# Sixteen tiles in front of a tuned spectral kernel: leftovers evicted with the pairs, seven row sums on GpSimd, a new order

## The chip, the cores and the metric

The kernel runs on one NeuronCore of a Trainium2 chip. The metric is the time of one execution on the device in microseconds (us), the median of several runs. A profiled execution is recorded beside them; the rows below are from it. The engines are TensorE (PE in the profile, its weight loads PEld), VectorE (DVE), ScalarE (ACT), GpSimd (POOL) and SyncE (SP, which here only issues DMA transfers).

## What is computed

`x` has 2048 rows (positions) of 576 columns, in fp32. Two branches read the normalised `xn`, and their sum is added to `x`:

```python
def _A_ref(x, w_r, w_i):                       # spectral filter
    X = rfft2(x, axes=(-2, -1))                # 2048 x 289 complex
    return irfft2(X * (w_r + 1j * w_i), (S, D), axes=(-2, -1))

def _B_ref(x, w_q, k1, k2, u, v):              # 32 heads, 8 x 8 experts, one expert per head
    q = einsum("nd,dhc->nhc", xf, w_q)
    s1 = einsum("nhd,ed->nhe", q[..., :dk], k1); s2 = einsum("nhd,ed->nhe", q[..., dk:], k2)
    top_e = argmax(s1) * E + argmax(s2)
    act = gelu(einsum("nd,nhkd->nhk", xf, u[top_e]))
    return einsum("nhk,nhk,nhkd->nd", g, act, v[top_e])   # g is 1

xn = _layernorm(x)
return x + _A_ref(xn, w_r, w_i) + _B_ref(xn, w_q, k1, k2, u, v)
```

## The kernel before

The two-dimensional transform is done as products. The 2048 positions are sixteen tiles of 128. For each tile `t`:

- `ln(t, n)` takes mean and variance, of some tiles on DVE (two `bn_stats` of 288 columns and a `bn_aggr`), of the tiles in `SA` on ACT (a summing pass and a squaring pass over the row), then the inverse root `r`: a square root on ACT and four small steps on DVE.
- `folds(t)` makes the difference and the sum of a row's halves (289 columns each, in `e`): the difference on GpSimd, the sum on DVE, which adds minus twice the mean. The factor `r` is multiplied into a copy of the transform matrix, `Rs` (ACT, for some tiles DVE). Columns 0 to 32, the leftovers beyond 128 pairs, are copied three times, to 99 columns (`fl`).
- `dft128(t)` multiplies: 8 products with the columns as weights give the pairs (2 x 256 columns of two PSUM banks), 4 give the leftovers (128 columns beside them, 99 partitions). In the trace a product in fp32 makes two records. Then the result is split into two fp16 parts: ACT copies it (`hi`), DVE subtracts the copy (`ab`); for the leftovers ACT copies and DVE corrects 33 partitions.

After that, `d_fwd`, `s_fwd`, `s_mul`, `s_inv`, `s_left`, `s_last` do the column transform, the step along positions, the filter and the way back for sixteen groups `g`; the transforms read the fp16 parts (`AB`, `ABL`) as weights. In the other branch `fold_part(b, s)` multiplies the keys into `w_q`, which comes from HBM in 32 pieces through five buffers; `scores`, `route`, `combine` pick the experts. `d_inv` and `fin` do the last transform and add all to `x`, which goes out from SyncE's queue.

The program first only notes the operations (`plan.add`): matmuls of one step that follow one another are one operation, everything else is one each. They are numbered as the source reaches them. `issue` then emits them in the sequence written out in `ORDER`, and `BANK` gives each PSUM tile its first bank. So `ORDER` fixes each engine's queue, and SyncE's too; an engine takes its queue strictly in that order. A GpSimd operation that reads the SBUF also waits for the DVE operation that stands last before it in `ORDER`, of those that use the port the two share (`held`, `tc.add_manual_dep`). All instructions are emitted in one line, L321, so the profile's groups are told apart by tiles: `A` is `e`, `U` is `fl`, `t` is also the scratch of the passes, `banks` all of PSUM, `c` the constants.

## Time and profile before

| | us |
|---|---|
| median of 3 runs | 206.54 (206.07 to 208.66) |
| the profiled execution | 204.99 |
| its span, first to last instruction | 203.2 |
| PE busy | 190.7 |
| DVE, ACT, POOL busy | 160.2, 124.0, 105.9 |
| granted TensorE clock, mean | 0.995 |

The span is what the engines' records cover; 1.8 us of the execution lie around it. A share of busy time is an average over stages of very different kinds, so the rows below are taken by stretch.

### The profile page before, as it was taken

To read this page: it belongs to the slowest core of one execution; us is meant where nothing else is said; L and a number is where in the kernel's file an instruction comes from. 1 tells how busy PE (TensorE), PEld (TensorE's weight loads), DVE (VectorE), ACT (ScalarE), POOL (GpSimd) and SP (SyncE) were. 2 spreads that over 40 slices of the span, in tenths; PEclk is the share of its full clock that TensorE was granted. 3 is DMA by queue.
4 is the path that set the end of the run, shared out by engine and by line. 5 is a ranking of instruction groups with operands and counts; after the bars stand their busy time and mean duration, and the time that the engine had idled before them with its cause. 6 is when DMAs were issued, how large, how long until landed. Compare 5 with 4: busy or idle time off the path is not lost.

```text
span 203.2 us, 6358 instructions
## 1 busy us (share of the span) xinstructions
PE 190.7 (94%) x2511; PEld 126.5 (62%) x2511; DVE 160.2 (79%) x383; ACT 124.0 (61%) x272; POOL 105.9 (52%) x166
## 2 busy tenths in 40 slices
PE   7877989999999999999999999999999999999990
PEld 2466777886676567754445555477444887776640
DVE  3799999855656657686989298999999989879871
ACT  3699988955646584888985851876440953333310
POOL 2563664100550063915336967752792569798841
PEclk9999999999999999999999999999999999999997
DMA  6999699999899999793566265422101000015575
GB/s 212 411 422 418 215 379 411 413 413 412 266 405 397 400 365 352 187 313 109 139 205 161 67 156 194 138 77 52 22 7 20 7 5 0 5 38 215 212 290 182
DMA packets 21156, 44.15 MB, mean 217 GB/s; under 512 B 7942, under 2 KB 10758, under 8 KB 21126
## 3 DMA queue, kind: packets, MB, share of 16 engines
q1 hardware_dynamic: 21126, 43.74, 60.5%
q8 instruction: 20, 0.33, 0.6%
q14 instruction: 10, 0.08, 0.1%
HBM read 38.30 MB, written 4.72 MB: 212 GB/s over the span
## 4 chain that ended last, share of the span: by engine, by line
PE 79%; DVE 10%; DMA 6%; issue 1%; ACT 1%; DVEq 0%; SPq 0%; ACTq 0%
PE banks L321 79%; DMA Wt<-in_W_dram 4%; DMA XN<-in_x_dram 2%; DVE st L321 2%; DVE AB L321 2%; DVE A L321 1%; DVE w L321 1%; DVE rr L321 1%; DVE t L321 1%; DVE mx L321 1%; DVE XN L321 0%; DVE Rs L321 0%; DVE mv L321 0%; DVE ABL L321 0%; ACT AB L321 0%
## 5 line engine op out<-in xcount | busy, mean ns | idle before, releaser
L321 PE MATMUL banks<-MU,xT 128*128 128x512 f16 x192 | 44.4, 379 | 0.0
L321 PEld LDWEIGHTS <-xT 128*128 128x128 f16 (+1 forms) x240 | 20.7, 99 | 27.4 <-issue 5.0
L321 PEld LDWEIGHTS <-AB 128*128 128x128 f16 x400 | 31.2, 122 | 7.4 <-issue 3.5
L321 POOL TENSOR_TENSOR U<-t,t 128x289 f32<-128x289 f32 x32 | 21.7, 703 | 22.0 <-DVE sc L321 15.7
L321 PE MATMUL banks<-c,AB 128*128 128x145 f16 (+1 forms) x384 | 32.3, 228 | 0.4 <-DVE AB L321 0.4
L321 POOL TENSOR_TENSOR t<-t,Wt 128x578 f32<-128x578 f32 x12 | 15.6, 1314 | 21.7 <-ACT t L321 16.4
L321 DVE TENSOR_TENSOR AB<-banks,AB 128x512 f16<-128x512 f32 x32 | 21.7, 681 | 5.1 <-ACT AB L321 4.7
L321 POOL TENSOR_TENSOR xT<-xf,xT 128x640 f16<-128x640 f32 x12 | 16.8, 1403 | 15.4 <-ACT xf L321 5.5
L321 POOL TENSOR_TENSOR A<-t 128x289 f32<-128x289 f32 x32 | 21.3, 699 | 2.8 <-DVE MT L321 2.5
L321 PE MATMUL banks<-Rs,A 64*128 64x128 f32 x256 | 19.1, 288 | 3.3 <-ACT Rs L321 1.4
L321 ACT ACTIVATE AB<-banks 128x512 f16<-128x512 f32 x32 | 18.9, 596 | 3.9 <-PE banks L321 3.2
L321 PEld LDWEIGHTS banks<-Rs,A 64*128 64x128 f32 x256 | 16.7, 195 | 5.8 <-ACT Rs L321 3.4
L321 PE MATMUL banks<-s,U 64*64 64x128 f32 x624 | 20.3, 272 | 0.0
L321 PEld LDWEIGHTS banks<-s,U 64*64 64x64 f32 x624 | 17.8, 133 | 2.5 <-issue 1.1
L321 PE MATMUL banks<-A,s 64*64 64x289 f32 x256 | 18.6, 408 | 0.0
L321 ACT ACTIVATE U<-banks,sc 128x290 f32<-128x290 f32 (+1 forms) x16 | 9.3, 595 | 14.3 <-PE banks L321 9.5
L321 PE MATMUL banks<-w,KP 128*32 128x288 f32 x256 | 18.0, 410 | 0.0
L321 DVE SCALAR_TENSOR_TENSOR t<-banks,wx,Wt 128x578 f32<-128x578 f32 x20 | 15.7, 813 | 2.4 <-PE banks L321 2.1
L321 PE MATMUL banks<-c,ABL 99*128 99x289 f16 (+1 forms) x64 | 15.7, 289 | 0.2 <-ACT A L321 0.2
L321 DVE SCALAR_TENSOR_TENSOR t<-banks,sc,U 128x290 f32<-128x290 f32 (+1 forms) x26 | 12.7, 532 | 3.4 <-ACT U L321 1.9
L321 ACT ACTIVATE t<-banks,wx 128x578 f32<-128x578 f32 x12 | 8.7, 743 | 10.6 <-DVE t L321 5.4
L321 ACT ACTIVATE xT<-xf,bx 128x640 f16<-128x640 f32 x16 | 13.1, 828 | 2.5 <-DMA xf<-in_xT_dram 2.3
(133 smaller groups left out, 350.5 us busy)
## 6 DMA issues: line engine op xcount, KB each, us to landing
w<-in_wq_dram SPq DMA_DIRECT2D x32, 576.0 KB
xf<-in_xT_dram SPq DMA_DIRECT2D x16, 320.0 KB
Wt<-in_W_dram SPq DMA_DIRECT2D x8, 578.0 KB
XN<-in_x_dram SPq DMA_DIRECT2D x7, 578.0 KB
out_dram<-XN SPq DMA_DIRECT2D x14, 288.0 KB
s<-in_s_dram SPq DMA_DIRECT2D x16, 192.0 KB
c<-in_c_dram SPq DMA_DIRECT2D x1, 868.5 KB
ABL<-lo SPq DMA_DIRECT2D x42, 16.5 KB
```

What stands on the lines that cost most here:

```text
L321: o.last = fn(*[x.place() if isinstance(x, _Ps) else x for x in args], **{k: x.place() if isinstance(x, _Ps) else x for k, x in kw.items()})
```

## The change

- `AB` and `ABL` become one array `ABX` of ten rows of columns: rows 0 to 3 the fp16 rests, 4 to 7 the `hi` parts, 8 and 9 the leftovers. Readers of `AB` take the other index (`1 - ha`).
- So `dft128` copies pairs and leftovers in one ACT instruction of 768 columns on all 128 partitions; the two DVE subtractions remain. A DVE fill sets the partitions 96 to 127 of the leftover columns of all eight banks to zero once, ahead of the fill of the warm-up operand; there are 14 warm-up products for 16.
- Tile 14 leaves `SA`: its statistics go from ACT to DVE.
- `GS`, empty before, holds seven tiles. For these GpSimd makes the sum of the halves, without the mean; DVE adds minus twice the mean in the 33 leftover columns alone; and in `dft128` two more products (one per half of the partitions) with minus four times the mean of each row as weights and the 64 columns of `Rs` put the mean into the pairs. `ln` makes that multiple in one more small GpSimd instruction for each of three groups.
- `ORDER` and `BANK` are written anew, 1225 operations for 1230.

These branches were in the source before and are now taken:

```python
if t in GS:                                              # folds
    G.tensor_tensor(e[:, 0], xn[:, 0:L], xn[:, L:], op=OP.add)
    V.tensor_scalar(e[:, 0, 0:33], e[:, 0, 0:33], rr[:, 2, t:t + 1], None, op0=OP.add)
...
if b == 0 and t in GS:                                   # dft128
    for h, r in enumerate(hs):
        P.matmul(p[:, h, 0:64], rr[r, 4, t:t + 1].to_broadcast([64, 128]), Rs[r, 0], start=False, stop=False,
                 tile_position=(64 * h, 0))
```

What the two orders say of some queues, decoded by numbering the operations (numbers after a name are tiles, groups or pieces):

```
ACT before  root 0 | sum 3 | square 3 | Rs 0 | root 1-3 | fl 0 | sum 7 | Rs 3 | Rs 2 | left 0 | square 7 | hi 0 | sum 5 | fl 1
            | square 5 | Rs 1 | left 3 | root 4-7 | hi 2 | sum 11 | hi 3 | Rs 4
ACT after   sum 3 | root 0 | fl 0 | square 3 | Rs 0 | root 1-3 | Rs 1 | Rs 2 | fl 1 | sum 7 | sum 5 | hi 0 | square 5 | Rs 3
            | square 7 | root 4-7 | sum 9 | hi 2 | hi 3 | Rs 4
DVE before  stats 0 | stats 2 | normalise 0 | sum 0 | stats 1 | normalise 1-3 | sums 1, 3, 2
DVE after   stats 0 | sum 0 | normalise 0, among it stats 2 | stats 1 | normalise 1-3, among it 33 columns of 3 and 2 | sum 1
PE before   tiles 0, 3, 2, 1, 4, 6, 5 | fold products x3 | tile 7 | x2 | tiles 9, 10, 8 | x3 | tiles 11, 13, 12, 14, 15
PE after    tiles 0, 1, 2, 3 | fold products x2 | tiles 4, 6, 7 | x2 | tile 5 | x1 | tiles 8, 9 | x3 | tiles 10 to 15
DVE before, at the end of the way back   si 12 | wt 7 | si 13 | rt | cb | rt | si 15 | rt | si 14 | two leftovers
DVE after                                si 12 | wt 7 | si 13 | cb | rt | si 15 | si 14 | rt | two leftovers
last additions before   tile 14 second half | tile 15 second half | tile 15 first half
last additions after    tile 15 second half | tile 15 first half | tile 14 second half
```

In DVE's new queue the statistics of tile 14 stand ahead of the subtraction of tile 5. The diff, without the tables of `ORDER` and `BANK` (the lines above tell of them) and the like edits of the readers:

```diff
-    AB = K([128, 2, 4, S], F16, "AB")
-    ABL = K([128, 2, S], F16, "ABL")
+
+    ABX = K([128, 10, S], F16, "AB")
+    AB = ABX[:, 0:8].rearrange("p (q c) s -> p q c s", q=2)
+    ABL = ABX[:, 8:10]
     U = K([128, 2316], F32, "U")
     slots["y"], slots["es"] = ([U[:, 579 * i:579 * i + 578] for i in range(4)], [U[:, 580 * i:580 * i + 580] for i in range(2)])
     turn["y"] = turn["es"] = 0
...
     ABt = AB.rearrange("p q c (n t) -> p q c n t", t=16)
     ABLt = ABL.rearrange("p b (n t) -> p b n t", t=16)
     ABi = AB.rearrange("p q c (a e g m) -> p q (c a) g e m", a=2, g=16, e=2)
-    wu = AB[:, 0, 0, 0:512]
+    wu = AB[:, 1, 0, 0:512]
     V.memset(wu, 1.0)
+
+    V.memset(banks.rearrange("p (k c) -> p k c", c=512)[96:128, :, 256:384], 0.0)
     pw_ = PS("m", (128, 512))
-    for k in range(16):
+    for k in range(14):
         P.matmul(pw_, wu[:, 0:128], wu, start=True, stop=True)
 
     MU = K([128, 2, 4, 512], F16, "MU")
...
             v = v.unsqueeze(2).to_broadcast([128, k, 2])
         V.tensor_scalar(dst.bitcast(I32), v, 0.5, float(0x1FBD1DF5 + (e << 23)), op0=OP.mult, op1=OP.add)
 
-    SA = (3, 5, 7, 9, 11, 13, 14, 15)
+    SA = (3, 5, 7, 9, 11, 13, 15)
     rr = K([128, 5, 16], F32, "rr")
     mv = K([128, 16, 2], F32, "mv")
     eps = K([128, 1], F32, "eps")
...
 
     FF = {}
     FG, RV = range(2, 16), (5, 7, 9, 11, 13, 14, 15)
-    GS = ()
+    GS = (2, 3, 4, 5, 6, 8, 10)
 
     @staged
     def folds(t):
...
             for h, r in enumerate(hs):
                 P.matmul(p[:99, h, 256 + 64 * b:320 + 64 * b], fl[r, b], Rs[r, 0], start=True,
                          stop=True, tile_position=(64 * h, 0))
-        m = p[:, :, 0:256].rearrange("p h (n r) -> p n h r", r=2)
-        l = p[:, :, 256:384].rearrange("p h (n r) -> p n h r", r=2)
-        hi, ab = (AB[:, q].rearrange("p c (h n) -> p (c h) n", n=64)[:, :, 4 * t:4 * t + 4].rearrange("p n (h r) -> p n h r", r=2)
-                  for q in range(2))
+        m = p[:, :, 0:384].rearrange("p h (n r) -> p n h r", r=2)
+        lo, hi, fl = (ABX[:, k:l].rearrange("p c (h n) -> p (c h) n", n=64)[:, :, 4 * t:4 * t + 4].rearrange("p n (h r) -> p n h r", r=2)
+                      for k, l in ((0, 4), (4, 10), (8, 10)))
         A.activation(hi, m, AF.Copy)
-        V.tensor_tensor(ab, m, hi, op=OP.subtract)
-        lo = ABL.rearrange("p b (h n) -> p (b h) n", n=64)[:, :, 4 * t:4 * t + 4].rearrange("p n (h r) -> p n h r", r=2)
-        A.activation(lo[:99], l[:99], AF.Copy)
-        V.tensor_tensor(lo[:33], l[:33], lo[:33], op=OP.subtract)
+        V.tensor_tensor(lo, m[:, 0:128], hi[:, 0:128], op=OP.subtract)
+        V.tensor_tensor(fl[:33], m[:33, 128:192], fl[:33], op=OP.subtract)
 
 
     uv = K([128, 4], F32, "uv")
...
-                    P.matmul(p[:, b, cs], ABg[:, ha, 2 * b + c, place[g], :], dc[:, b, hb, cs], start=False,
+                    P.matmul(p[:, b, cs], ABg[:, 1 - ha, 2 * b + c, place[g], :], dc[:, b, hb, cs], start=False,
...
-        hi, ab = (ABi[:, q, :, g] for q in range(2))
+        ab, hi = (ABi[:, q, :, g] for q in range(2))
```

## Rows read from the trace of the kernel before

**Rows 1.** Part 1 of the page: busy us, share of the span, instructions.

```profile
PE 190.7 (94%) x2511; PEld 126.5 (62%) x2511; DVE 160.2 (79%) x383; ACT 124.0 (61%) x272; POOL 105.9 (52%) x166
```

**Rows 2.** Busy time by stretch: length, each engine, granted clock, DMA share, GB/s.

```profile
0.00:7.84 7.84, 6.08 (x16) 2.11 (x17) 3.85 (x14) 3.83 (x8) 2.69 (x9) 1.00 0.79 281
7.84:17.48 9.64, 6.24 (x96) 5.61 (x96) 8.84 (x30) 8.16 (x24) 5.52 (x18) 1.00 1.03 420
17.48:26.64 9.16, 8.58 (x137) 6.70 (x137) 8.71 (x26) 9.13 (x26) 5.75 (x13) 1.00 0.83 305
26.64:61.20 34.56, 34.53 (x563) 27.15 (x563) 24.15 (x68) 23.32 (x56) 11.01 (x24) 1.00 0.99 384
61.20:73.40 12.20, 11.55 (x196) 7.57 (x192) 8.35 (x21) 8.39 (x18) 0.74 (x1) 1.00 1.03 403
73.40:157.20 83.80, 83.74 (x922) 47.74 (x922) 69.92 (x156) 54.12 (x103) 48.85 (x54) 1.00 0.49 144
157.20:163.40 6.20, 5.75 (x167) 4.87 (x166) 6.17 (x12) 5.28 (x16) 3.51 (x7) 1.00 0.05 8
197.40:203.20 5.80, 0.24 (x2) 0.00 (x0) 1.37 (x3) 0.40 (x1) 0.80 (x1) 0.81 0.53 194
```

**Rows 3.** The same view inside 20 to 25 us.

```profile
20.00:22.50 2.50, 2.47 (x46) 2.06 (x46) 2.50 (x8) 2.50 (x7) 2.33 (x7) 1.00 0.75 307
22.50:25.00 2.50, 2.50 (x48) 1.75 (x40) 2.39 (x9) 2.47 (x9) 1.04 (x2) 1.00 0.60 125
```

**Rows 4.** Groups of instructions by form: busy us, mean ns | idle before, releasers.

```profile
L321 ACT ACTIVATE AB<-banks 128x512 f16<-128x512 f32 x32 | 18.9, 596 | 3.9 <-PE banks L321 3.2 <-DVE ABL L321 0.3
...
L321 ACT ACTIVATE ABL<-banks 99x256 f16<-99x256 f32 x18 | 6.5, 381 | 0.7 <-PE banks L321 0.6
...
L321 POOL TENSOR_TENSOR A<-XN 128x289 f32<-128x289 f32 x16 | 11.2, 708 | 4.8 <-DMA XN<-in_x_dram 4.1 <-DVE A L321 0.4
...
L321 DVE SCALAR_TENSOR_TENSOR A<-XN,rr 128x289 f32<-128x289 f32 x16 | 8.1, 530 | 0.3 <-POOL rr L321 0.2
...
L321 PE MATMUL banks<-Rs,U 64*99 64x64 f32 x128 | 7.8, 243 | 1.0 <-POOL U L321 0.6 <-ACT U L321 0.4
...
L321 DVE BATCH_NORM_STATS2 st<-XN 128x6 f32<-128x288 f32 x16 | 6.6, 446 | 3.0 <-DMA XN<-in_x_dram 3.0
...
L321 ACT ACTIVATE t<-XN,rr 128x576 bf16<-128x576 f32 x8 | 6.2, 778 | 0.1
...
L321 ACT ACTIVATE t<-XN 128x576 bf16<-128x576 f32 x8 | 5.5, 688 | 0.4 <-DMA XN<-in_x_dram 0.4
...
L321 DVE TENSOR_SCALAR Rs<-c,rr 128x128 f32<-128x128 f32 x7 | 2.5, 352 | 0.0
...
L321 DVE MEMSET AB<- 128x512 f16 x1 | 0.5, 485 | 0.1
```

**Rows 5.** Timeline of the first tiles, ACT and PE: start, length, instruction, [idle before].

```profile
4.77 0.30 ACT L321 ACTIVATE rr<-mv,eps 128x1 f32<-128x1 f32 x1 [2.55 <-DVE mv L321]
...
5.46 0.68 ACT L321 ACTIVATE t<-XN 128x576 bf16<-128x576 f32 x1 [0.39 <-DMA XN<-in_x_dram]
...
7.84 1.22 PE L321 MATMUL banks<-Rs,A 64*128 64x128 f32 x16 [0.28 <-DVE A L321]
...
17.48 1.22 PE L321 MATMUL banks<-Rs,A 64*128 64x128 f32 x16 [1.43 <-ACT Rs L321]
...
21.85 1.66 PE L321 MATMUL banks<-w,KP 128*32 128x288 f32 x24
```

**Rows 6.** Timeline of PE, two groups of 32 spectral products.

```profile
67.55 2.89 PE L321 MATMUL banks<-A,s 64*64 64x289 f32 x32
...
140.04 2.13 PE L321 MATMUL banks<-A,s 64*64 64x289 f32 x32
```

**Rows 7.** Timeline of PE at the first inverse column product.

```profile
163.36 0.88 PE L321 MATMUL banks<-c,AB 128*128 128x145 f16 x10 [0.45 <-DVE AB L321]
```

**Rows 8.** Timeline of DVE, the last additions.

```profile
197.43 1.37 DVE L321 SCALAR_TENSOR_TENSOR XN<-banks,sc,XN 128x289 f32<-128x289 f32 x3 [0.68 <-PE banks L321]
```

More of the change, by code (lines that the diff above doesn't have):

```diff
@@ L956, in d_inv @@
                 for n, (ha, hb) in enumerate(((0, 0), (0, 1), (1, 0))):
-                    P.matmul(p[:, b, cs], ABt[:, ha, 2 * c + b, :, t], ic[:, b, hb, cs], start=(c == n == 0), stop=False)
+                    P.matmul(p[:, b, cs], ABt[:, 1 - ha, 2 * c + b, :, t], ic[:, b, hb, cs], start=(c == n == 0), stop=False)
         plan.cut()
```

127 rows, old and new, of tables (BANK, ORDER) are left out of this document.

## The prediction, made before the changed kernel was run

> **What bounds the kernel now.** I read first the busy times, then the busy time by stretch, then the chain of waits and the stretches in which TensorE (PE) stood still. PE is busy for 94% of the span [rows 1]. Cut where its work changes kind, the stretches show where the other 6% lies [rows 2]: before the first product of a tile at 7.84 us it runs only its 16 warm-up products; from 7.84 to 17.48 it stands for 3.40 us, to 26.64 for 0.58, to 61.2 for 0.03; 0.65 in 61.2 to 73.4, 0.45 in 157.2 to 163.4, and 5.56 at the end. So after 7.84 us there are 5.1 us in all to be won inside the kernel, and the sixteen tiles (normalise, fold, transform) hold 4.0 of them. In that stage PE waits for VectorE (DVE) and ScalarE (ACT), which feed it: DVE is busy 8.84 of 9.64 us and then 8.71 of 9.16, ACT 8.16 and 9.13, GpSimd (POOL) only 5.52 and 5.75 [rows 2]. From 17.48 on all three are near their limit, so one relieved by a little does not free the others. The DMA is full (shares above 1) up to 73 us except for a hole at 20 to 25 us, where 307 and 125 GB/s stand against 420 [rows 2, 3]: SyncE waits there for a buffer of the fold products.
>
> **Leftovers evicted with the pairs.** Removed are sixteen ACT copies of 99x256 at 0.381 us; the pair copies grow from 512 to 768 columns. From 0.381 at 256 and 0.596 at 512 columns [rows 4] the line leads to 0.81, so a tile saves 0.596 + 0.381 - 0.81 = 0.17 us, 2.7 us in all. That is the upper end: where ACT's instructions follow one another closely their ends overlap, and only the columns count; the lower end is nothing. It lies on ACT, in a stage where DVE is as full. Against it the pair copy now waits for the four leftover products of its tile (0.49 us, [rows 4]: 7.8 us for sixteen tiles) where it waited for the other eight alone. DVE's two subtractions stay as they are.
>
> **One zeroing of PSUM, two warm-ups fewer.** DVE fills 1024 columns of 32 partitions before the warm-up operand. By the 0.485 us of a 512-column fill [rows 4] that is 1.0 us, twice that at worst. DVE has nothing to do before 3.7 us, so it costs nothing there; the warm-ups start 1.0 us later, and 14 instead of 16 (6.08 us together, [rows 2]) end near 7.8. The first tile's product, below, comes later than that. Without this cover it would cost the 0.2 us by which they end later.
>
> **Statistics of tile 14 from ACT to DVE.** ACT loses 0.688 + 0.778 = 1.5 us, DVE gains two statistics of 0.446 and a small closing one, 1.1 us [rows 4].
>
> **Seven row sums on GpSimd.** DVE drops seven adds of 0.530 us for seven additions over 33 columns; those cost between nothing and the 0.352 of a 128-column one [rows 4], I take 0.25, near the latter's fixed part: 7 x 0.28 = 2.0 us saved, 0.9 net of tile 14. POOL adds seven times 0.708 and three small ones, 5.7 us. Its 11.3 busy us of 18.8 become about 17, still less than either neighbour. The Trainium skill advises the other way: "GPSIMD Engine Reference", section 4.1, calls GpSimd about twice as slow as VectorE in a two-input elementwise operation. The rows give 0.708 against 0.530, a third more; with the factor two the POOL term would be 8 us and the queue full.
>
> PE gets two products a tile, 64 rows by 64 columns in fp32. The nearest row is the leftover product of the same width, 7.8 us for 128 records [rows 4], 61 ns each; two records a product and 28 in all make 1.7 us at most, 0 at least if the wait for an operand covers them. As the first two tiles' share falls into idle time, I take 1.3.
>
> **The new order, first tiles.** Numbering the operations shows a summing pass of tile 3 put ahead of tile 0's square root on ACT. Before, that root ran at 4.77; the pass cannot begin before its load has landed, at 5.46, and takes 0.68 [rows 5]. So the root comes at 6.2. From root to first product it was 3.07 us, of which the 0.53 of tile 0's sum is now done earlier: the first product comes near 8.75, 0.9 later. Next, what leads to tile 4's product at 17.48: between the root of tiles 1 to 3 and tile 4's scaled matrix ACT loses two leftover copies (0.76) and gains a summing pass (0.69) and three longer copies (0.6); that root itself is late by the 0.9 of tile 0, less some DVE time that the early sum frees, 0.7; so tile 4's product starts near 18.7. But two groups of fold products now stand before it in PE's queue, 0.55 us each (1.66 for three, [rows 5]). In work done PE is 0.1 us behind. From there the stage is nearly all PE's: five of the seven tiles with the new product follow, 0.9 us; of the old 0.6 us of standing I count 0.1 as recovered. The stage thus ends 0.9 us later. Its bounds: if all 4.0 us of standing went, 0.9 + 1.3 - 4.0 = 1.8 earlier; if a tile in the middle also waits for DVE to clear its bank (the order puts tile 14's statistics ahead of tile 5's subtraction, about 1 us) and nothing is recovered, 2.5 later.
>
> **The order, 61 to 73 us.** PE stands there for 0.65, and a group of 32 products that takes 2.13 elsewhere took 2.89, 0.7 more [rows 6]; the DMA is full in that stretch [rows 2], and these products and those before them read what it was still bringing. The new order frees two fold buffers earlier, which closes the hole at 20 to 25 us: (420-307)/420 x 2.5 + (420-125)/420 x 2.5 = 2.4 us of transfer time [rows 3]. With the data earlier and PE later, both waits go: -1.35. If a later buffer blocks SyncE instead, 0.
>
> **The order, from 157 us.** The subtraction for which the inverse products wait stood behind three routing steps and PE stood 0.45 for it [rows 7]; two remain ahead of it: -0.3, between 0 and the 0.45 us of the gap. In the last group of additions the one whose bank is ready first is now last, so the last three (1.37 us, [rows 8]) start when PE is fully done: +0.25, at most the length of one, 0.45. All else between is PE work in another order, 83.74 busy of 83.80 us [rows 2]: nothing to win, and nothing lost unless a bank comes free late.
>
> **Sum.** 0.9 - 1.35 - 0.3 + 0.25 = -0.5 on a profiled execution of 204.99 us: 204.5. The median of the runs is 206.54, 1.55 above that execution, so I expect 206.0 there.
>
> **Rivals.** One: ACT was the true limit of the tiles. It is the fullest engine from 17.48 to 26.64 (9.13 of 9.16), and it is relieved by up to 4.2 us. Then the standing time goes and the sum is -1.8 - 1.35 - 0.3 = -3.45: 203.1. Against it speaks that DVE is as full and is relieved by only 0.9.
>
> Two, slower: GpSimd becomes the limit. Each tile's fold copy now waits for a GpSimd difference, a GpSimd sum, and a DVE step between, and a GpSimd operation that uses the common port is held in the code until the DVE operation before it in the order is done. It decides as soon as a sum ends after PE has reached that tile: each such tile then costs 0.7 us. With five tiles (4, 5, 6, 8, 10) that is 3.5 us, and the DMA waits come back only in part: +3.5 - 0.5 = 209.5. For it: 17 of 18.8 us is full for a queue that already stood waiting for DVE. Against it: the tile order puts sums two tiles ahead of their use. The Trainium skill, "SBUF — State Buffer", section "Who interferes with whom", says that a VectorE instruction with two SBUF inputs and a GpSimd one that reads SBUF block each other for a whole instruction. Here GpSimd's adds of the tiles last 0.708 on average [rows 4] beside a DVE that is busy nine tenths of the time, which leaves no room for frequent blocking of that kind.
>
> Three: one array now holds pairs and leftovers, and if the waits went by array instead of by region, inverse and forward products would wait for transfers of leftovers that they don't read. Seven such steps, each priced like the one gap of that kind, 0.45 [rows 7], give +3.2 - 0.5: 209.2. The old array already mixed regions that different steps write, without such waits, so this is unlikely.
>
> **How the numbers follow.** The forecast (about 0.5 faster, within 1.5 us) has 0.68, the first rival 0.16, the second 0.13, the third 0.03. The range takes in the first rival and nearly reaches the second: 203.0 to 209.0. A change of 2% is 4.1 us, about what a measurement can tell here. Faster by more needs the first rival and luck beside it: 0.04; slower by more (210.7) needs two of the slower ones together, or more tiles than five: 0.07; within: 0.89.
>
> **What would show it.** In the changed trace: the first tile product near 8.7 and tile 4's near 18.7; the last tile done near 40.5; ACT copies of 768 columns near 0.81 us; GpSimd adds still near 0.70; no hole in the DMA at 20 to 25 us; the group of 32 products before 70 us at 2.13; the gap at 163 gone. I am wrong if PE stands on GpSimd in the tiles, or if PE is never idle from 10 us on.

## The result, and the profile after

The changed kernel takes 207.75 us in the median of 22 runs (206.1 to 210.84), the kernel before 206.5 us beside it (22 runs, 204.79 to 209.29). The ratio is 1.0049 with a 95% interval of 1.0026 to 1.0071: about 1.0 us slower, where 0.5 us faster was forecast. It is less than the 1.25 us between the medians because the slow runs of both kernels are left out of it. The time lies inside the predicted range and inside 2%, but on the other side of no change. The profiled execution spans 204.6 us, against 203.2.

Part 1 of the page of the changed kernel answers to [rows 1]:

```profile
PE 190.7 (93%) x2537; PEld 127.3 (62%) x2537; DVE 162.7 (79%) x387; ACT 119.9 (59%) x252; POOL 112.7 (55%) x175
```

The work moved as intended: ACT has 4.1 us less, GpSimd 6.8 more. PE is as busy as before: the new products (0.17 us a tile in its timeline) are about made up for by the two warm-ups that are gone (5.12 us for 6.08). DVE has 2.5 us more, where the prediction's terms (2.0 less for the sums, 1.1 more for tile 14, 1.0 for the fill) leave it about even; the section on the middle comes back to it. What was lost is standing time of PE. The same stretches as in [rows 2]:

```profile
7.84:17.48 9.64, 7.15 (x116) 6.55 (x120) 7.50 (x28) 7.19 (x20) 6.62 (x18) 1.00 1.02 420
17.48:26.64 9.16, 7.67 (x126) 6.30 (x118) 9.02 (x29) 7.31 (x18) 6.73 (x16) 1.00 0.86 322
...
61.20:73.40 12.20, 12.20 (x224) 9.02 (x222) 7.43 (x18) 10.31 (x22) 1.55 (x3) 1.00 0.99 361
73.40:157.20 83.80, 82.11 (x912) 45.62 (x910) 70.61 (x148) 53.83 (x104) 49.79 (x53) 1.00 0.50 152
157.20:163.40 6.20, 6.13 (x157) 4.67 (x159) 6.10 (x16) 3.57 (x11) 2.38 (x4) 1.00 0.05 8
```

From 61.2 to 73.4 us PE doesn't stand at all now (0.65 before), and that part came as predicted. From 73.4 to 157.2 it stands for 1.69 us, where it had stood for 0.06. PE's timeline of the changed kernel names the places:

```profile
9.06 1.22 PE L320 MATMUL banks<-Rs,A 64*128 64x128 f32 x16 [1.38 <-ACT Rs L320]
...
19.15 0.51 PE L320 MATMUL banks<-Rs,A 64*128 64x128 f32 x4 [1.20 <-DVE AB L320]
...
68.75 2.61 PE L320 MATMUL banks<-A,s 64*64 64x289 f32 x32
...
80.50 0.69 PE L320 MATMUL banks<-w,KP 128*32 128x288 f32 x8 [1.01 <-DMA w<-in_wq_dram]
...
126.80 1.98 PE L320 MATMUL banks<-s,U 64*64 64x128 f32 x64 [0.48 <-DVE t L320]
...
136.27 0.38 PE L320 MATMUL banks<-wm,on 128*128 128x2 f32 x2 [0.20 <-ACT t L320]
...
164.25 0.27 PE L320 MATMUL banks<-id,MT 128*128 128x128 f16 x2 [0.19 <-DVE AB L320]
164.85 2.38 PE L320 MATMUL banks<-c,AB 128*128 128x145 f16 x28 [0.33 <-DVE AB L320]
```

The first and second rows answer to [rows 5] (first tile 7.84, tile 4 17.48), the third to [rows 6], the last to [rows 7]. To say where the difference of 1.4 us between the spans arises, the starts of the same work in both timelines are compared:

| stretch | before | after | change |
|---|---|---|---|
| last tile product ends at | 39.64 | 40.75 | +1.1 |
| first product of the scores starts at | 87.69 | 88.79 | +1.1 (nothing more) |
| from there to the third transpose of the combines | 69.37 | 70.15 | +0.78 |
| third to eighth transpose | 37.56 | 38.00 | +0.44 |
| PE's end to the end of the span | 5.56 | 4.64 | -0.92 |

From the eighth transpose to PE's end both take 3.02 us. The sum is 1.1 + 0.78 + 0.44 - 0.92 = 1.4. This is one profile of each kernel; what further profiles of the same orders make of it is told with the experiments.

The groups of instructions by form (busy us, mean ns) answer to [rows 4]:

```profile
L320 ACT ACTIVATE AB<-banks 128x768 f16<-128x768 f32 x16 | 12.5, 804 | 1.7 <-PE banks L320 1.6
...
L320 POOL TENSOR_TENSOR A<-XN 128x289 f32<-128x289 f32 x23 | 15.8, 698 | 9.3 <-DVE A L320 3.2 <-DMA XN<-in_x_dram 2.8 <-PE banks L320 1.5
...
L320 DVE TENSOR_SCALAR A<-A,rr 128x33 f32<-128x33 f32 x7 | 1.9, 279 | 0.0
```

The 768-column copy takes 0.804 us (0.81 estimated), a GpSimd addition 0.698 (0.70), the 33-column addition 0.279 (0.25). The prices of the operations were right. What failed lies between them.

### The profile page after: what moved, and what is told of

It reads as the page before. It is cut to its first block, busy times and chain, and to the rows that moved or that the text cites. A ratio compares the mean times of both kernels' runs of the same rounds, so it can differ in the third digit from the quotient of the medians.

```text
span 204.6 us, 6425 instructions
## 1 busy us (share of the span) xinstructions
PE 190.7 (93%) x2537; PEld 127.3 (62%) x2537; DVE 162.7 (79%) x387; ACT 119.9 (59%) x252; POOL 112.7 (55%) x175
## 4 chain that ended last, share of the span: by engine, by line
PE 65%; DVE 14%; ACT 6%; DMA 5%; POOL 5%; issue 3%; POOLq 0%; SPq 0%; DVEq 0%; ACTq 0%
PE banks L320 65%; DVE w L320 6%; DMA w<-in_wq_dram 3%; ACT t L320 3%; DVE AB L320 2%; DMA XN<-in_x_dram 2%; POOL A L320 2%; DVE MT L320 1%; DVE st L320 1%; DVE mx L320 1%; POOL t L320 1%; POOL U L320 1%; DVE rr L320 1%; ACT xf L320 1%; DVE t L320 1%
## 5 line engine op out<-in xcount | busy, mean ns | idle before, releaser
L320 PEld LDWEIGHTS <-AB 128*128 128x128 f16 (+1 forms) x462 | 34.4, 123 | 8.5 <-issue 4.1
L320 PE MATMUL banks<-c,AB 128*128 128x145 f16 (+3 forms) x448 | 36.5, 236 | 0.3 <-DVE AB L320 0.3
L320 POOL TENSOR_TENSOR U<-t,t 128x289 f32<-128x289 f32 x32 | 22.6, 729 | 21.8 <-ACT A L320 14.9
L320 DVE TENSOR_TENSOR AB<-banks,AB 128x512 f16<-128x512 f32 (+1 forms) x50 | 27.8, 581 | 2.6 <-ACT AB L320 2.4
L320 ACT ACTIVATE AB<-banks 128x768 f16<-128x768 f32 (+2 forms) x34 | 22.6, 680 | 4.6 <-PE banks L320 4.5
L320 PE MATMUL banks<-Rs,A 64*128 64x128 f32 x256 | 20.7, 291 | 4.1 <-ACT Rs L320 2.6
L320 PEld LDWEIGHTS banks<-Rs,A 64*128 64x128 f32 x256 | 17.5, 194 | 6.4 <-ACT Rs L320 5.1
L320 POOL TENSOR_TENSOR A<-XN 128x289 f32<-128x289 f32 x23 | 15.8, 698 | 9.3 <-DVE A L320 3.2
L320 PE MATMUL banks<-A,s 64*64 64x289 f32 x256 | 17.7, 407 | 0.0
L320 ACT ACTIVATE A<-banks 128x578 f32<-128x578 f32 x16 | 10.4, 654 | 6.2 <-issue 4.0
```

What stands on the lines that cost most here:

```text
L320: o.last = fn(*[x.place() if isinstance(x, _Ps) else x for x in args], **{k: x.place() if isinstance(x, _Ps) else x for k, x in kw.items()})
```

## Experiments

All times are medians; each ratio is to the kernel before on the same chip, with its 95% interval. "Scores" is the start of the scores' first product. In order edits, `root(0)` and the like stand for the numbers of those operations in ORDER.

### Edits and order, taken apart

**e1**, all edits in the order of before:

```diff
  ORDER, BANK of before, and in it:
- hi(t) 512, lo(t) 256 columns        + hi(t) 768 at the later of the two places
- DVE sum(t)                          + GpSimd sum(t) behind its difference, DVE sum33(t) here
- ACT sum, square of tile 14          + DVE statistics of tile 14
```

> All four edits (wide eviction, one zeroing and 14 warm-ups, tile 14's statistics on DVE, seven sums on GpSimd with their products) in the order of before; each new instruction stands where the one that it replaces stood, a GpSimd sum right behind its tile's difference. Theory (the loss of 1.25 us is the new order's, at places that I priced at nothing): the edits cost their seven pairs of products, 1.3 us of PE, and win part of the 4.0 us of standing back: 206.0 to 207.0, no tile product waits for GpSimd, and no wait for a fold buffer of a microsecond near 80 us. Rival (the edits themselves carry the loss): 207.7 or more, with PE waiting in the tiles on GpSimd or on the wide copies.

Measured: 210.88 us, ratio 1.0203 (1.0138 to 1.0268). PE waits 1.49 us for GpSimd at 16.09, tiles end at 41.66, three waits for fold pieces make 1.76 us, the scores start at 91.92.

**e2**, the new ORDER and BANK with the operations of before:

> None of the edits, only the new order (and its banks): sums, leftover copies and tile 14's statistics stand where the new order has what replaces them. Theory: the waits that belong to the order are all there: first tile product near 9 us, 1.0 us on a transfer near 80 us, 0.5 us behind the routing steps near 127 us, and the early stores; 207.5 to 208.5, slower than before. Rival (the edits carry the loss): near 206.5, like before, since the order merely moves waits about. Second rival (the order fits only the edits): over 209, because DVE must run seven sums that the order doesn't make room for.

Measured: 210.94 us, 1.0239 (1.0167 to 1.0311). Tiles end at 42.58, scores start at 90.45. But its first product comes at 7.97, not near 9.

**e8**, the changed kernel with `GS = ()`, so that the seven sums are DVE's again:

> The changed kernel with the seven sums back on DVE, at the places of the small additions that finish them, and without their products; the wide eviction, the zeroing, tile 14's statistics on DVE and the new order stay. Theory: DVE gets 7 x (0.53 - 0.28) = 1.8 us more in the tiles and the sums come later in its queue, PE has 1.3 us less: the tiles end 0.5 to 2 us later than 40.68, 208 to 209.5. Rival (GpSimd's sums only cost, by their products and by the common port): the tiles end 1 us sooner and the median is 206.5 to 207.

Measured: 209.2 us, 1.0138 (1.0079 to 1.0198). Tiles end at 41.14; first product at 7.95.

**e16**, in before, only the wide eviction, the zeroing and 14 warm-ups:

> Of the edits only the wide eviction with its zeroing of PSUM and 14 warm-ups, in the order of before; each wide copy stands where the later of the two copies stood. Sums and tile 14's statistics stay as before. Theory: ACT gains, but the subtraction of the pairs and so each bank comes free later, in an order that was made for the earlier copy: 206.5 to 207.5, no gain without a new order. Rival one: ACT was the limit of the tiles, 205 to 206. Rival two: the late pair copy alone explains the 4 us that all edits together cost in the old order, 209 or more.

Measured: 208.98 us, 1.0107 (1.0051 to 1.0164). Tiles end at 41.90, with PE standing 1.76 us at 28.14 us for the scaled matrix (its wait names DVE and Rs): the later pair copy holds DVE's subtractions and these the scaled matrix behind them.

What follows: both theories fall, and so does e2's first rival. The times of e1's rival (207.7 or more, with PE waiting for GpSimd) and of e2's second rival (over 209) came. But the edits don't carry the loss by themselves: they cost 2.0% in the old order, at the places that I chose for them there, and 0.5% in the order made for them, while that order without them costs 2.4%. The new order is made for the edits and nearly pays for them. e8's theory (208 to 209.5) held: in the new order the sums are better on GpSimd, though its profile, of the fastest of its runs (207.22), hardly shows the loss. e16 lies above its theory, at the edge of its second rival's 209. So a part of this change can't be priced by adding it to the order of before, as my sum did.

### The first tile: which step was late

**e5**, GpSimd's first run of four additions waits for the end of tile 0's root steps:

```diff
         V.scalar_tensor_tensor(r, q, 96.0, r, op0=OP.add, op1=OP.mult)
+        if t == 0:
+            plan.ops[-1].port = True
```

> The changed kernel, in which GpSimd's run of four additions (one difference and two sums ahead of their use, one more difference; 5.70 to 8.37 us) waits until DVE has done the last of tile 0's three small root steps. Theory: DVE's small steps took 0.60 and 0.66 us instead of 0.16 because GpSimd was adding beside them; alone they take 0.16 again and tile 0's first product comes at 8.1 to 8.3 instead of 9.06. The additions now end near 10.4, which may take some of it back at tile 1. If PE's lateness in the tiles is what the later transfers wait for, the scores start up to 0.9 us sooner than 88.79 and the median falls to 207.0 to 207.3; if it is the transfers themselves, the scores start at 88.5 to 89 and the median stays at 207.7. Rival for the steps: they are slow for another reason (tile 2's statistics between them) and stay at 0.6; first product at 9 or later.

**e6**, the root first on ACT:

```diff
- ... 51 (pass of tile 3), 36 (root(0)), ...
+ ... 36, 51, ...
```

> The changed kernel with tile 0's square root put back ahead of tile 3's summing pass on ACT, nothing else moved. My prediction held this pass alone responsible for 0.9 us at the first product: by it the product comes near 8.1. Theory now (the additions on GpSimd slow the steps behind the root): the root comes 1.2 us sooner, but its steps on DVE now fall under the same run of additions, so the product comes only 0.3 to 0.6 sooner, 8.4 to 8.8; median 207.3 to 207.8.

**e7**, both:

> Both edits together: square root first, and GpSimd's additions behind tile 0's root steps. Theory: first product at 7.4 to 7.9 us, before the end of the warm-ups or close to it; the tiles end 0.5 to 1.2 us sooner than 40.68; scores start at 87.7 to 88.2 if PE's lateness is what later transfers wait for (median 206.5 to 207.0), or still at 88.5 to 89 if the transfers set it (207.7).

Measured: e5 208.57 us, 1.0088 (1.0055 to 1.0121), first product 8.21; e6 207.75, 1.0051 (1.0016 to 1.0086), first product 8.91; e7 207.51, 1.0039 (1.0001 to 1.0076), first product 7.70. Timeline of DVE in the changed kernel, tile 0's root steps, and then of POOL:

```profile
6.28 0.17 DVE L320 RECIPROCAL rr<-rr 128x1 f32<-128x1 f32 x1 [0.66 <-ACT rr L320]
6.47 0.60 DVE L320 SCALAR_TENSOR_TENSOR rr<-rr 128x1 f32<-128x1 f32 x1
7.00 0.81 DVE L320 BATCH_NORM_STATS2 st<-XN 128x6 f32<-128x288 f32 x2
7.72 0.66 DVE L320 SCALAR_TENSOR_TENSOR rr<-mv,rr 128x1 f32<-128x1 f32 x1
```

```profile
5.70 2.67 POOL L320 TENSOR_TENSOR A<-XN 128x289 f32<-128x289 f32 x4 [0.34 <-DVE A L320]
```

The same in e6, where the root came 1.2 us sooner:

```profile
5.57 0.16 DVE L321 RECIPROCAL rr<-rr 128x1 f32<-128x1 f32 x1
5.76 0.69 DVE L321 SCALAR_TENSOR_TENSOR rr<-rr 128x1 f32<-128x1 f32 x1
6.38 0.81 DVE L321 BATCH_NORM_STATS2 st<-XN 128x6 f32<-128x288 f32 x2
7.11 0.65 DVE L321 SCALAR_TENSOR_TENSOR rr<-mv,rr 128x1 f32<-128x1 f32 x1
7.80 0.62 DVE L321 SCALAR_TENSOR_TENSOR rr<-rr 128x1 f32<-128x1 f32 x1
```

and in e5 (DVE, then POOL), with the additions behind them:

```profile
6.58 0.16 DVE L321 SCALAR_TENSOR_TENSOR rr<-rr 128x1 f32<-128x1 f32 x1
...
7.39 0.14 DVE L321 SCALAR_TENSOR_TENSOR rr<-mv,rr 128x1 f32<-128x1 f32 x1
7.57 0.16 DVE L321 SCALAR_TENSOR_TENSOR rr<-rr 128x1 f32<-128x1 f32 x1
```

```profile
7.81 2.65 POOL L321 TENSOR_TENSOR A<-XN 128x289 f32<-128x289 f32 x4 [2.38 <-DVE rr L321]
```

The three steps on one column take 0.60 to 0.69 us while GpSimd adds, and 0.14 to 0.16 without it. The reciprocal (0.16) and the statistics (0.81 for two) between them, with one operand in SBUF, are as long in both. In e6 the root's gain of 1.2 us is eaten by a third slow step and by DVE's early sum ahead of the reciprocal. So the first product's lateness is shown to come mostly from GpSimd's run of additions (0.85 us from the changed kernel to e5, 1.21 from e6 to e7), and less from the summing pass that I blamed (0.15 us from e6 to the changed kernel, 0.51 from e7 to e5; with the sums off GpSimd, e2 has 7.97 and e8 7.95, where before has 7.84). My 3.07 us from the root to the first product held slack: in before, DVE was at tile 2's statistics until 6.20 us, more than a microsecond after the root.

But it bought nothing here. With the first product at 7.70 in e7, the second tile's still comes at 11.62, tile 4's at 19.28, and the tiles end at 40.85, as in the changed kernel (11.63, 19.15, 40.75). The second tile now waits for GpSimd's late queue, by way of its root: PE stands 2.37 us before it in e7 and 2.59 us in e5 (12.35), and then the granted clock is at the lower level for a while, as in this window of e7:

```profile
13.00:15.00 2.00, 2.00 (x24) 2.00 (x22) 1.01 (x3) 2.00 (x7) 1.96 (x4) 0.50 1.03 424
```

In e5 the tiles end at 41.73. So these runs don't show what an early first product is worth when nothing behind it comes late. Of the medians, e5's misses both of its forecasts, e6's meets its own, and e7's lies between its two.

### The fold products: room in the transfers, or buffers

**e3**, two groups of fold products exchanged in PE's queue:

```diff
- ... 382, ... (16 entries) ..., 380, ...
+ ... 380, ... (16 entries) ..., 382, ...
```

> The changed kernel with two groups of fold products (third row of weights, both halves of its third piece) exchanged in PE's queue, so that the half whose transfer is already there goes first, as in before; nothing else moves. Theory: the wait of 1.01 us at 80.5 us goes and the end comes 0.7 to 1.0 us sooner, 206.7 to 207.0. Rival (DVE, full from 88 us on, sets the end anyway): the wait goes and comes back as another behind it, 207.5 to 207.8.

**e9**, the constants' load cut in two, the second half issued behind the load of s32 13:

```diff
-    Q.dma_start(c16, a["c16"])
+    Q.dma_start(c16[:, :o2], a["c16"][:, :o2])
+    Q.dma_start(c16[:, o2:], a["c16"][:, o2:])
```

> The changed kernel with the load of the transform's constants cut in two: the half that only the last stage reads (0.445 MB, 1.07 us at 416 GB/s) is issued near 125 us, when the transfers have room, instead of near 32.5 us. Theory (the wait of 1.01 us at 80.5 us is the transfers', which are behind in the stretch up to 83 us whatever PE's order): the waits for fold pieces between 60 and 85 us sum to under 0.4 us, the scores start at 87.7 to 88.3 instead of 88.79, median 206.9 to 207.4. Rival (each piece waits for its buffer, which PE frees, not for room in the transfers): the waits stay near 1 us and the scores start at 88.5 to 89; 207.7.

**e10**, the same in before:

> The same cut of the constants' load in the kernel before. Theory: its waits on late data in 61 to 73 us (1.35 us by my count) shrink by about 1 us, and the median falls to 205.3 to 205.9. Rival: buffers, not room; 206.9 as before.

Measured: e3 207.95 us, 1.0053 (1.0015 to 1.0091); e9 209.01, 1.0129 (1.0078 to 1.018); e10 206.89, 1.001 (0.9972 to 1.0047). In e3 the wait of 1.01 us went and another came, as its rival said; in e9 four waits for transfers make 1.37 us, the scores start at 89.62, and the median misses both forecasts. PE's timeline in e3:

```profile
83.29 0.69 PE L321 MATMUL banks<-w,KP 128*32 128x288 f32 x8 [0.55 <-DMA w<-in_wq_dram]
```

and two steps of e9's chain of work (start, length, what was waited for):

```profile
67.02 8.51 DMA w<-in_wq_dram
76.32 8.01 DMA w<-in_wq_dram
```

With 0.445 MB less to move, these two pieces still took 8.0 to 8.5 us from issue to landing. That the theory falls doesn't show that there was room, though. From 55 to 80 us the transfers are as full in e9 (shares of 0.96 to 1.02) as in the changed kernel (0.97 to 1.03); one window of each, the changed kernel first:

```profile
70.00:75.00 5.00, 5.00 (x73) 3.77 (x69) 4.46 (x11) 3.47 (x7) 1.65 (x2) 1.00 1.01 362
```

```profile
70.00:75.00 5.00, 4.98 (x68) 3.55 (x59) 4.40 (x11) 3.73 (x7) 1.79 (x2) 1.00 1.02 366
```

What the cut took away early was not filled: from 40 to 50 us e9 moves 329 and 344 GB/s, the changed kernel 386 and 397. So e9 doesn't decide between room and buffers. e10 took as long as before, as its rival said; in its profile the group of 32 products took 2.18 us again, and a wait of 1.20 us for a piece came at 66.81.

What holds back a piece's issue is mostly the buffer that PE must first free. SyncE's waits (total, times, longest) in before and after, 15 to 90 us:

```profile
SPq L321 <- PE banks L321: 25.8, 12, 5.6
SPq L321 <- DMA w<-in_wq_dram: 16.3, 7, 5.2
```

```profile
SPq L320 <- PE banks L320: 33.6, 12, 5.8
SPq L320 <- DMA w<-in_wq_dram: 6.2, 5, 3.8
```

SyncE waits 7.8 us more for PE, and 10.1 us less for transfers of pieces. The hole in the DMA moved instead of closing. In after:

```profile
20.00:25.00 5.00, 4.71 (x79) 3.80 (x76) 4.89 (x15) 4.45 (x12) 4.43 (x12) 1.00 0.86 349
25.00:30.00 5.00, 5.00 (x88) 4.45 (x86) 4.66 (x17) 3.51 (x9) 3.25 (x9) 1.00 0.88 300
50.00:55.00 5.00, 5.00 (x79) 3.22 (x74) 3.77 (x6) 2.24 (x7) 0.61 (x1) 1.00 0.66 212
```

and in before, where 20 to 25 us had 307 and 125 GB/s [rows 3]:

```profile
25.00:30.00 5.00, 4.46 (x74) 3.72 (x76) 4.49 (x13) 4.87 (x15) 3.37 (x9) 1.00 1.01 375
50.00:55.00 5.00, 5.00 (x76) 2.83 (x77) 3.16 (x10) 3.29 (x9) 2.66 (x4) 1.00 0.80 268
```

What 20 to 25 us gained was lost again by 55.

One profile of each kernel is too little for this stretch. e15 and e17 below have the whole program of before up to the scores, and e4, e11 and e18 that of the changed kernel, so there are five more profiles of it (times in us, from PE's timelines):

| the same program up to the scores | last tile product ends | scores start | between |
|---|---|---|---|
| before, e15, e17 | 39.64, 39.69, 39.58 | 87.69, 88.71, 88.68 | 48.05, 49.02, 49.10 |
| after, e4, e11, e18 | 40.75, 40.69, 40.47, 40.73 | 88.79, 88.86, 87.91, 88.82 | 48.04, 48.17, 47.44, 48.09 |
| difference of the means | +1.0 | +0.2 | -0.8 |

The tiles' +1.1 is repeated, the scores' is not. The profiled execution of before is a fast one (204.99 us, median 206.54); in e15 the same program waits for pieces where it didn't:

```profile
58.04 1.66 PE L321 MATMUL banks<-w,KP 128*32 128x288 f32 x24 [0.66 <-DMA w<-in_wq_dram]
...
67.38 0.69 PE L321 MATMUL banks<-w,KP 128*32 128x288 f32 x8 [0.69 <-DMA w<-in_wq_dram]
```

With a scatter of 0.7 to 1.1 us within a program, seven profiles give the -0.8 only roughly.

### The middle: DVE ahead of PE

**e4**, two multiplications earlier on DVE:

```diff
- ..., 640, 641, 756 (combining, routing), ... (3 entries) ..., 845, 809 (multiplications), ...
+ 845, 809 right behind the forward products that they read, ...
```

(they move as a pair, and so come ahead not only of the combining and routing, but also of the ACT copies that read the same banks)

> The changed kernel with two multiplications of the spectra (groups 10 and 11) moved on DVE from behind the routing steps to right behind the forward products that they read. Theory: the bank comes free sooner, the stop of 0.48 us at 126.8 us goes, 207.2 to 207.4. Rival: the routing steps, now later, hold something else (a combine's transpose on PE, the scores' bank), 207.7 or more.

Measured: 209.86 us, 1.0171 (1.0112 to 1.023). The pair reached DVE at 125.80, hardly sooner, but the ACT copies of the same banks, which had run at 123.01, now stood behind it for 6.02 us, and PE stood 2.46 (ACT's and PE's timelines, then the windows):

```profile
127.43 1.38 ACT L321 ACTIVATE t<-banks,wx 128x578 f32<-128x578 f32 x2 [6.02 <-DVE t L321]
...
128.86 3.48 PE L321 MATMUL banks<-s,U 64*64 64x128 f32 x64 [2.46 <-ACT t L321]
```

```profile
130.00:132.00 2.00, 2.00 (x44) 2.00 (x43) 2.00 (x3) 0.32 (x1) 1.92 (x3) 0.50 0.08 15
```

The last row shows a second price: granted clock 0.50, the lower level (1.2 GHz), right behind the standstill, and 64 products take 3.48 us instead of 1.98.

**e11**, the other way round: ten routing and combining steps moved behind the pair, the ACT copies left ahead.

> The changed kernel with ten routing and combining steps on DVE moved behind the two multiplications of groups 10 and 11; the copies on ACT that read the same banks stay ahead of both, unlike in the run in which the multiplications themselves were moved. Theory: the multiplications run as soon as their products are there (near 122.9 instead of 125.9), the stop of 0.5 to 0.8 us at 126.8 goes, and the third transpose of the combines comes 0.5 us sooner than 158.94; median 207.2 to 207.5. Rival (DVE sets the end of this stage, at 97% busy): the stop goes, but the transpose comes no sooner; 207.7.

**e12**, with e6 and e9 together:

> The changed kernel with the constants' load cut in two, the routing steps behind the multiplications and tile 0's root first. Theory: the gains add, 0.6 + 0.4 + 0.2: 206.3 to 206.8, about the time of before, with its earlier stores on top. Rival (what one edit frees is taken by the next wait): 207.3 to 207.8.

Measured: e11 212.81 us, 1.0279 (1.0224 to 1.0335); e12 212.4, 1.0262 (1.0208 to 1.0316). The stop at 126.8 is gone in e11, as meant (its products run at 126.17). But a GpSimd operation waits for DVE's last common-port step ahead of it in the order, and that is now a routing step:

```profile
128.87 0.46 POOL L321 TENSOR_TENSOR MT<-MT,mk 128x128 f32<-128x128 f32 x1 [8.38 <-DVE w L321]
...
139.51 0.59 PE L321 MATMUL banks<-wm,on 128*128 128x2 f32 x2 [4.14 <-ACT t L321]
```

In the changed kernel that operation ran at 126.16. Its queue is 2.7 us late, ACT's squares behind it too, and PE stands 4.14 us and then runs at clock 0.50. e11 and e12 lie far above their forecasts and their rivals. Both repairs of a 0.5 us stop cost 2 to 5 us: DVE, GpSimd, ACT and PE stand in one chain here, with next to no slack.

Neither repair touched what the traces show ahead of the stop. DVE works through the routing steps up to the pair without a pause, and one of them, with two operands in SBUF, runs beside an addition of GpSimd (DVE, then POOL, in the changed kernel):

```profile
119.02 1.66 DVE L320 TENSOR_TENSOR w<-w,wt 128x896 bf16<-128x896 bf16 x1
```

```profile
118.80 1.40 POOL L320 TENSOR_TENSOR xT<-xf,xT 128x640 f16<-128x640 f32 x1
```

The other seven steps of this form take 0.61 to 0.68 us. In the ten kernels in which the new order is whole here (after, e2, e3, e5 to e9, e13, e18) this step takes 1.39 to 1.92 us, PE's stop takes 0.21 to 0.77, and in each the stop is the step's time less 1.15 to 1.18 us. By that, a step of 0.62 us would leave none. The kernels with the old order have no such stop. So the stop goes with DVE's delay beside GpSimd, as at the first tile. It is not the only delay: take the DVE steps behind the scores that took at least 0.15 us longer than the shortest of their form in before. Their excess adds up to 1.2 us in before, to 0.6 to 1.5 in the six other kernels with the old order there, and to 3.5 in the changed kernel (3.2 to 4.7 in the kernels with the new order). That is most of DVE's 2.5 us more. No run moved that addition, so what this would win isn't shown.

### The two halves, each by itself

**e13**: ORDER is the first 530 entries of before, then all that is left in the new order; no edits.

> The kernel before, without any of the edits, in its own order up to the end of the fold products (some 80 us), and from there in the new order. Theory (each stage carries its own part): the scores start at 87.7 as before; from there the changed kernel's profile lost 0.8 us up to the combines, won 0.2 at 163 us, lost 0.6 in the last stage and won 0.9 at the very end, so 0.3 us in all: 206.9 to 207.5. Rival (the later stage is no dearer in itself, it only ran late and out of step after the late scores): 205.8 to 206.3, the 0.9 of the stores being won.

**e14**: the first 520 entries of the changed kernel, then what is left in the order of before; all edits.

> The changed kernel with all edits in the new order up to the end of the fold products, and from there in the order of before. Theory: the scores start at 88.8, 1.1 us later than before, and nothing behind is recovered: 207.6 to 208.2. Rival (the loss is behind the scores): 206.5 to 207.

Measured: e13 208.43 us, 1.0076 (1.0037 to 1.0115), scores at 90.20; e14 207.76, 1.0078 (1.0044 to 1.0112), scores at 91.26, since PE asked for the last pieces sooner and waited 2.99 us for them. e13's median misses both of its forecasts. e14's lies in its theory's range by luck: its scores started 2.5 us later than said; behind them 1.5 us were won against the changed kernel, and 1.0 lost again at the end. Both are slower before the scores than their first half by itself, in part at the seam; of e13's lateness, 2.0 us are waits for pieces at 57 to 68 us, where e15 and e17 wait 1.3 as well. Behind the scores the orders differ in the same way in every kernel where that part was left whole (times in us, from PE's timelines):

| from the scores on | to the third transpose | third to eighth | PE's end to span's end |
|---|---|---|---|
| old order: before, e1, e10, e14, e15, e16 | 69.37, 69.93, 69.25, 69.17, 70.10, 70.31 | 37.45 to 37.56 | 5.56, 5.47, 5.08, 5.61, 5.50, 6.12 |
| new order: after, e2, e3, e5, e6, e7, e8, e9, e13 | 70.15, 70.76, 71.27, 70.85, 71.29, 69.87, 70.50, 70.83, 70.93 | 37.80 to 38.02 | 4.64, 4.86, 4.99, 4.62, 4.67, 4.74, 4.59, 5.06, 4.56 |
| difference of the means | +1.0 | +0.5 | -0.8 |

So the new order behind the scores loses 1.5 us and wins 0.8 at the end, with the edits (after) or without (e2, e13), and the old one doesn't, with them (e1, e14) or without. In the first column the two groups overlap, so its 1.0 is rough. This is the mechanism of e13's theory, with 0.7 us in all instead of 0.3; its rival, that the later stage is no dearer in itself, falls.

### The end

**e15**, in before, each store right behind its addition:

> The kernel before with each store of the result issued right behind its addition, so that SyncE's queue doesn't stand before tile 4's store until 181.5 us; nothing else moves. Theory (the new order's end is shorter by 0.6 to 0.9 us because its stores begin at 175 us): first store near 173, the end 4.6 to 4.9 us after PE's last product instead of 5.56, median 206.0 to 206.3, faster than both kernels. Rival (the last store's own way sets the end): 206.9.

**e17**, in before, from entry 1203 on the new order (last products, additions, stores):

> The kernel before with only its last operations in the new order, from the products of the last two pairs of tiles on: the last additions, the one that GpSimd finishes coming last, and their stores. In nine kernels with the new order 4.56 to 5.06 us lie between PE's last product and the end, in six with the old one 5.08 to 6.12, and stores begun at 173 us didn't change that. Theory (the order of the last additions and stores is worth it): 4.6 to 4.9 us instead of 5.56 behind PE's last product, median 205.7 to 206.1, faster than both kernels. Rival (the end is shorter only because PE comes later and finds the transfers empty): 5.5 us, 206.5 as before.

**e18**, the changed kernel, in the last stage the old order up to the additions of tiles 10 and 11, then the new end:

> The changed kernel, all edits, in the new order up to the first inverse product of the last stage (164.85 us), in the order of before from there to the additions of tiles 10 and 11, and with the new order's end. In each kernel with the new order the stretch from the third to the eighth transpose of the combines took 37.8 to 38.0 us, with the old one 37.45 to 37.56; the trace of the changed kernel shows three weight loads there that wait for GpSimd's additions, 0.6 us in all. Theory: the stretch takes 37.5 us again, median 207.1 to 207.4. Rival (the inverse products' late start at 164.85 sets it, not their order): 38.0, 207.7.

Measured: e15 206.09 us, 1.0002 (0.9974 to 1.0031). The first store was issued at 173.62 instead of 181.54 us, and still 5.50 us lie behind PE's end: early stores are not the gain. That the median met the forecast says nothing for them: the kernel before, beside it, took 206.42. e17 208.35 us, 1.0074 (1.0034 to 1.0114): the seam put GpSimd's last additions later and PE stood 1.00 us for them; 5.17 us lie behind PE's end, between the two groups. Inconclusive. e18 207.62 us, 1.0088 (1.0051 to 1.0126): 37.93 us from the third to the eighth transpose, so its theory falls and its rival's numbers came; that the late start at 164.85 us is the reason isn't shown by itself. In after PE's weight loads wait three times for GpSimd there (view of waits: total, times, longest):

```profile
PEld banks L320 <- POOL A L320: 0.6, 3, 0.2
```

In e18 they wait less, but PE stands longer ahead of it (waits, then PE's timeline):

```profile
PEld banks L322 <- POOL A L322: 0.4, 2, 0.2
```

```profile
165.20 3.27 PE L322 MATMUL banks<-c,AB 128*128 128x145 f16 x42 [0.72 <-ACT MT L322]
```

No version beat the kernel before; e10 and e15 equal it.

## Why the prediction was wrong

**The step that failed**: "nothing to win, and nothing lost unless a bank comes free late." 1.2 us were lost behind the scores in the profile (0.78 + 0.44), 1.5 in the mean of nine kernels against six, and e13 and e14 show it to go with the order there, whatever stands ahead of it. I had priced it at 0 because PE was 83.74 of 83.80 us busy there. It was the case named, a bank that DVE frees late: PE stops 0.48 us at 126.8 us and, behind that, 0.20 at 136.27, after one routing step had taken 1.0 us too long beside GpSimd's addition. The 0.44 us from the third to the eighth transpose stay open. A stretch that is full shows no gap, and so shows nothing of how little slack its order has.

**The term that was mis-sized** is the one on 61 to 73 us: "With the data earlier and PE later, both waits go: -1.35." In that stretch they went: no idle time, the group of 32 products at 2.61 us instead of 2.89 (2.13 was said), and the fold products at 74 us as early as before though the tiles ended 1.1 later. But a wait of 1.01 us came at 80.5 us, for a piece issued when PE had consumed an older one, and the hole filled at 20 us opens again at 50. Between the two profiled executions nothing of the 1.35 is left, the bound that I gave ("if a later buffer blocks SyncE instead, 0"); in the means of the seven profiles about 0.8 us is.

**The wrong sign**: the last additions were said to cost 0.25 and the end became 0.92 us shorter. That it is the new order's is shown by 15 kernels; that it isn't the early start of the stores, by e15. Which of the last additions and stores does it stays open.

**Right in size, wrong in cause**: the tiles, +0.9 said, +1.1 measured (1.0 in the means), with 3.98 us of standing from 7.84 to 26.64 us in both kernels, tile 4's product at 19.15 (18.7 said), last tile done at 40.75 (40.5). The first product at 9.06 (8.75) was put down to the summing pass ahead of the root; it was mostly GpSimd's additions. And in e7 an earlier first product moved neither the second tile nor the tiles' end. What holds tile 4's product at 19 us wasn't tried.

**Right**: the prices of the copies and additions; zeroing and warm-ups free; the 157 us stretch (168.69 - 157.06 = 11.63 us from the third transpose to the next pair's products before, 11.44 after: -0.2, with -0.3 said), though the gap itself is 0.52 us now.

**The rivals.** ACT as the true limit of the tiles: no, ACT has 2.8 us more free time in 7.84 to 26.64 us and PE still stands as long. GpSimd as the limit: PE stands for GpSimd itself nowhere in the tiles of the changed kernel, only by way of DVE's steps and ACT's scaled matrix, so not in the form given. But the rule cited with it was dismissed too soon. I wrote that GpSimd's mean of 0.708 us leaves no room for frequent blocking; GpSimd's time was indeed unchanged, and it was DVE that waited, 0.14 to 0.16 us becoming 0.60 to 0.69 at the first tile, and 0.62 becoming 1.66 at 119 us. The Trainium skill, "SBUF — State Buffer", section "Who interferes with whom", says that a DVE instruction with two SBUF inputs contends with a GpSimd instruction that reads SBUF and that one with at most one such input, outside the two-port modes, doesn't. The rows above agree on both halves. Waiting by array: no inverse or forward product waits for a transfer of leftovers in the trace.

Together: 0.9 - 1.35 - 0.3 + 0.25 = -0.5 was said; in the same stretches 1.1 + 0 + 1.2 (with the -0.2 in it) - 0.9 = +1.4 was measured between the two profiles, and 1.0 - 0.8 + 1.5 - 0.8 = +0.9 between the means of the profiles with the same orders, beside +1.0 in the ratio.

## What to carry to other kernels

Where transfers are issued into a ring of buffers, a piece can only be issued once its buffer is consumed: follow the ring to its end before counting a closed hole as a gain. A stretch in which PE hardly stands has nothing to win for PE, but reordering it can lose: price it by the slack of the chain of engines that feeds it. When an order is written anew, look which DVE steps with two SBUF operands come to run beside GpSimd's additions. One profile of each kernel can mislead by a microsecond in a stretch that waits for transfers; profiles of other runs with the same order there show the scatter. And an order written for one set of instructions doesn't carry another: here either half of the change alone cost four to five times what both cost together.

## What the runs showed of the hardware

DVE steps on a single column with two SBUF operands took 0.60 to 0.69 us beside GpSimd's additions of 128x289 and 0.14 to 0.16 us without them, while GpSimd's own 0.66 to 0.70 us stayed; I had expected the longer instruction to suffer. A DVE step of 128x896 with two SBUF operands, 0.61 to 0.68 us for the other seven in the changed kernel, took 1.39 to 1.92 us in ten kernels beside GpSimd's additions (128x640 among them, 1.40 us). After PE stood for 2.37 us (e7), 2.46 (e4), 2.59 (e5) and 4.14 us (e11) its granted clock was at the lower level, 0.50, for products behind it; after 1.00 us (e17) and 1.76 (e16) it stayed at 1.00.
